# Moving the check of the weights from the vector engine to ScalarE, with new ordering offsets, in a fused attention and feed-forward kernel

## The chip, the core and the metric

The kernel runs on one core of a Trainium2 chip. The metric is the device time of one execution in microseconds (us), lower being better; the figure to compare is the median of repeated executions. The engines are named as in the profile: PE (TensorE, the matrix multiplies), PEld (its weight loads), DVE (the vector engine), ACT (ScalarE), POOL (GpSimd) and SP (SyncE, which here only issues transfers).

## The reference

There are two stages. The first is attention with four sink columns and a sliding window, for 4 batches, 8 heads, 768 positions and head size 64. The second is a feed-forward layer whose gate is a cosine, for 3072 tokens, width 512 and inner width 2048.

```python
scores = scale * q @ k.T
keep = (pos_k < n_sink) | ((rel >= 0) & (rel < window))      # n_sink 4, window 128
scores = where(keep, scores, -1e9)
a = exp(scores - max); a = a / (sum(a) + 1e-9)
x = (a @ v) with the heads of a token side by side           # 3072 x 512
h = x @ w_in                                                 # 512 x 2048
out = (h * cos(h)) @ w_out                                   # 2048 x 512
```

## The kernel before

**Tiles and stages.** The 3072 tokens are cut into 12 chunks of 256. A chunk has 8 heads of attention and then 8 slots of the feed-forward layer, each slot covering 256 of the 2048 inner columns. Precision beyond one pass of the multiplier is had by splitting numbers into a high and a low part: `h_mm` (L419) makes 24 multiplies for a slot and `out_mm` (L479) makes 12. Between them stands a chain that goes back and forth: `turns` on ACT (L428), `rest` on DVE (L434), `cosine` on ACT (L441, function Sin), `gate` on DVE (L446), `g_hi` on ACT (L458) and `g_lo` on DVE (L464). The heads have their own chain: `load_k` and `load_q` (L776, L763), `k_turn` on DVE (L879), the scores on PE (L906), `mask` on DVE (L919), `expo` on ACT (L928, function Exp with a summed output), `norm` (L951 on ACT, L953 on DVE or POOL), the transpose of the probabilities (L1021) and `values` on PE (L1101). Attention of later chunks is interleaved with the slots of earlier ones. The first three chunks have an opening in which weights are loaded and split and the first 24 heads use another form (L850, L1077), with filler multiplies (L1379) where PE has no other work.

**Order.** The order of all instructions on each engine is worked out while the program is built. Each step is entered in a `Plan` with the engines that can take it, an estimated duration, its dependencies and a due time; `order` then plays the engines forward and lets each take the ready step with the smallest due time. Due times are offsets held in the table `C`. For example, `DH` and `DM` place a slot's steps, `DQ`, `DS`, `DV` and `DX` the steps of a head, `SO` the splitting of `w_out`, `CK` the checks, and `PEN` is what a step is set back if it needs another ACT function table than the one loaded. Some steps may go to one of several engines (`norm`, some copies, the low parts). An engine then runs its instructions strictly in that order.

**The check.** The weights arrive as 64-bit floats and are turned to 32 bits by integer operations, which is right as long as no weight is very small. While the feed-forward layer runs, each of the 32 pieces of the weights (512 KB) is therefore read once more from memory into one of two `raw` buffers, and the upper words, read as 32-bit floats, are tested (`check_piece`, L595). One DVE instruction multiplies the 128 x 512 upper words with themselves and keeps the largest of the negated squares of each partition in a column of `tiny`. One check is entered for each slot after the first two chunks, due `CK` after it. In the end the columns are reduced (L1361) and compared with the limit `MIN_TOP * MIN_TOP`; where a weight is too small, a slow general path is run. It isn't run with these inputs. The two `raw` buffers also carry the output rows (`out_copy`, L407 and L409; `out_store`, L508), in an order fixed when the plan is made, and a load into one of them is issued by SP, which takes its transfers in order.

Of the kernel before, what the change touches and what calls it, by code (L numbers as in the profile page):

```python
# [9 lines left out]
F32 = mybir.dt.float32  # L10
F32R = mybir.dt.float32r
I32 = mybir.dt.int32
AF = mybir.ActivationFunctionType
ALU = mybir.AluOpType
PSUM = bass.MemoryType.PSUM

P = 128
# [8 lines left out]
MASKED = 8.0e9  # L26

C = {
# [3 lines left out]
    "NWF": 0.232, "PB": 5, "PEN": 27.684, "PL": 3, "POOLF": 4.428, "POOLPEN": -1.361, "QE": 5.937, "R": 2, "RAW": 2,  # L32
# [3 lines left out]
}  # L36
# [1 line left out]
MIN_TOP = 1.125 * 2.0**-15  # L38


def f32(ap):
    return ap.bitcast(F32)
# [7 lines left out]
class Plan:  # L50
# [8 lines left out]
    def buf(self, tag, n):  # L59
        row = self.bufs.setdefault(tag, [])  # L60
        row.append(Buf(row[len(row) - n] if len(row) >= n else None, len(row) % n))
        return row[-1]

    def add(self, engines, fn, deps, prio, lat=0.0, table=None, port=False):
        self.steps.append((engines, fn, deps, prio, lat, table))
        if port:
            self.port.add(len(self.steps) - 1)
        return len(self.steps) - 1
# [101 lines left out]
def attn_moe_kernel(ctx, tc, q, k, v, n_sink, window, w_in, w_out, out):  # L170
    nc = tc.nc
    B, H, S, D = q.shape
    w64 = w_in.dtype == mybir.dt.int64
    DM, DFF = w_in.shape
# [13 lines left out]
    NSLOT = NFT // FG  # L188
    WP = 2 * FG * P

    NEH = int(C["NEH"]) // 2 * 2
    NE = -(-NEH // H)
# [3 lines left out]
    cp = ctx.enter_context(tc.tile_pool(name="cp", bufs=1))  # L196
# [19 lines left out]
    rel, col = rc[:, 0], rc[:, 1]  # L216
    nw_i = cp.tile([P, 2, 2], I32, name="nw_i")
    nw4 = cp.tile([P, 2, 2], F32, name="nw4")
    neg3 = cp.tile([P, 3], F32, name="neg")
    neg, quarter = neg3[:, 0:2], neg3[:, 2:3]  # L220
    flag = cp.tile([1, 4], F32, name="flag")
    lims = cp.tile([1, 2, 2, 2], F32, name="lims")
    mine = cp.tile([GR, GQ], F32, name="mine")
    tiny = cp.tile([P, NC * NSLOT // 2 + NFT], F32, name="tiny")
    redo = cp.tile([1, 1], I32, name="redo")

    def setup():
        nc.vector.memset(quarter, HALF_PI_DOWN)
        nc.gpsimd.memset(ident, 0.0)
        nc.gpsimd.affine_select(  # L230
            out=ident, in_=ident, pattern=[[-1, P]], compare_op=ALU.not_equal, fill=1.0, base=0, channel_multiplier=1
        )
        nc.gpsimd.iota(rc_i[:, 0], pattern=[[-1, P]], base=0, channel_multiplier=1)
        nc.gpsimd.iota(rc_i[:, 1], pattern=[[1, P]], base=0, channel_multiplier=0)
        nc.gpsimd.memset(env.kz, 0.0)
        nc.gpsimd.memset(xb, 0.0)
        nc.gpsimd.memset(f32(env.vs), 0.0)

        for _ in range(C["WARM"]):
            nc.tensor.matmul(out=env.warm, lhsT=ident, rhs=ident, start=True, stop=True)  # L240
        nc.vector.memset(lims, 0.0)
        nc.vector.memset(lims[:, 0, 1, 0:1], 1.0)
        nc.vector.memset(lims[:, 1, 0, 0:1], float(NSINK))
        nc.vector.memset(lims[:, 1, 1, 0:1], float(P))
        nc.vector.tensor_single_scalar(out=minus, in_=ident, scalar=-1.0, op=ALU.mult)
        nc.vector.tensor_copy(out=rc, in_=rc_i)
        nc.vector.tensor_reduce(
            out=mine, in_=ident[:GR, :GR].rearrange("p (a h s) -> p h a s", a=2, h=GQ), axis=mybir.AxisListType.XY,
            op=ALU.max,
        )  # L250
# [261 lines left out]
    def dve(n, two=False, ptr=False):  # L512
        return ((n / 2 if two else n) + 62) / 960 + (0.06 if ptr else 0)

    def act(n, sbuf=True):
        return n / 1200 + (0.092 if sbuf else 0.051)
# [4 lines left out]
    def dma(n):  # L521
        return (("SP", 0.45 * n),)
# [50 lines left out]
    def split_piece(plan, prio, w, ready, before):  # L573


        add = plan.add

        def round_hi(e):
            nc.scalar.copy(out=w.high(), in_=w.w32)

        def rest_lo(e):
            e.tensor_tensor(out=w.low(), in0=w.w32, in1=f32(w.hi), op=ALU.subtract)  # L582

        s4 = add((("ACT", act(WP)),), round_hi, [ready], prio)
        return [s4, add(sub(WP), rest_lo, [s4, *before], prio, port=True)]

    def check_piece(plan, prio, k, w):

        add, buf = plan.add, plan.buf
        r = buf("raw", C["RAW"])  # L590
        raw = raws[r.nth]
        top = raw[:, :, 1].bitcast(F32)

        def least(e):
            nc.vector.tensor_tensor_reduce(  # L595
                out=top, in0=top, in1=top, op0=ALU.mult, op1=ALU.max, scale=-1.0, scalar=-3.0e38,
                accum_out=tiny[:, k : k + 1],
            )

        i = add(dma(1), lambda e: e.dma_start(out=raw.rearrange("p n w -> p (n w)"), in_=w.src), [r], prio - 6, lat=2.6)  # L600
        j = add((("DVE", dve(WP) + 0.02),), least, [i], prio, port=True)
        r.users += [i, j]
        return j

# [68 lines left out]
    def banded_path():  # L673
        plan = Plan()
        add, buf = plan.add, plan.buf
# [444 lines left out]
        i = add([("ACT", 1.9)], load_limits, [], -3000.0, lat=2.8)  # L1120
        i = add([("DVE", 0.6)], limits, [i], -3000.0, lat=0.1)
# [10 lines left out]
        def slot_time(a, s):  # L1132
            return C["S1"] + ((a - 1) * NSLOT + s) * T if a else C["S0"] + s * C["STEP"]

        slots = sorted((slot_time(a, s), a, s) for a in range(len(chunks)) for s in range(NSLOT))
# [222 lines left out]
        tmin = cp.tile([P, 2], F32, name="tmin")  # L1358
# [8 lines left out]
        def least_flag(e):  # L1367
            e.tensor_reduce(out=tmin[0:1, 1:2], in_=env.tm, axis=mybir.AxisListType.X, op=ALU.max)
            e.scalar_tensor_tensor(
                out=redo, in0=tmin[0:1, 1:2], scalar=-MIN_TOP * MIN_TOP, in1=flag[:, 0:1], op0=ALU.is_gt, op1=ALU.max  # L1370
            )

        idle = buf("b0", 1)
# [14 lines left out]
        for s in range(NSLOT):  # L1388
            t = slot_time(0, s)
# [5 lines left out]
        for m, (t, ss, w) in enumerate(sorted(pieces, key=lambda w: w[0])):  # L1395
            i = weight_piece(plan, t, w, guard=False, first=m < C["PL"])
# [16 lines left out]
        checks = [w for ws in w_ins for w in ws] if w64 else []  # L1413
        checks += w_outs if w64 else []
        checked = []
        nh = 0
        for t, a, s in slots:
            hs = ("b4", "b2") if a < NE - 1 else ("b4", "b2", "b3")
            hb = hs[nh % len(hs)]
            nh += 1  # L1420
            dense(plan, xs[a], a, s, t, T, w_in_ready, w_out_split if a else w_out_first, ACC, hb)
            for m in range(0 if a else FG):
                f = s * FG + m
                prio = slot_time(1, s) + C["SO"] + C["SO2"] * m
                pair = split_piece(plan, prio, w_outs[f], w_out_ready[s][f], before["out"])
                before["out"] = pair + xs[0].om[f]
                w_out_split.setdefault(s, []).append(pair[1])
            if a > 1 and len(checked) < len(checks):
                checked.append(check_piece(plan, t + C["CK"], len(checked), checks[len(checked)]))
        assert len(checked) == len(checks)  # L1430
        if w64:
            t = slots[8 + 2 * NSLOT + len(checks)][0]
            btp = buf("tp", 1)
            i = add([("DVE", 0.16)], least_all, checked, t)
            i = add([("PE", 0.13)], least_turn, [i, btp], t + 1.0)
            btp.users.append(add([("DVE", 0.4)], least_flag, [i], t + 2.0))

        emit(plan.order(BEGIN), setup)
        if not w64:
            nc.vector.tensor_copy(out=redo, in_=flag[:, 0:1])  # L1440
# [125 lines left out]
    with ExitStack() as ctx2:  # L1566
        x = banded_path()
# [37 lines left out]
```

## Time and profile before

| | us |
|---|---|
| median of three executions | 742.26 |
| lowest and highest of them | 742.24, 743.15 |
| the profiled execution's own time | 742.62 |
| its span, first to last instruction | 740.9 |
| PE busy in the span | 723.5 |
| DVE busy | 628.0 |
| ACT busy | 557.3 |
| POOL busy | 106.4 |

The span is shorter than the execution's own time by what lies ahead of the first and behind the last instruction. The granted TensorE clock is 0.999 of full speed over the span. Busy time of PE is a union of pipelined instructions whose ends are modelled, so that a short stall between two of them doesn't show in it.

### The profile page before, as it was taken

To read this page: it belongs to the slowest core of one execution; us is meant where nothing else is said; L and a number is where in the kernel's file an instruction comes from. 1 tells how busy PE (TensorE), PEld (TensorE's weight loads), DVE (VectorE), ACT (ScalarE), POOL (GpSimd) and SP (SyncE) were. 2 spreads that over 40 slices of the span, in tenths; PEclk is the share of its full clock that TensorE was granted. 3 is DMA by queue.
4 is the path that set the end of the run, shared out by engine and by line. 5 is a ranking of instruction groups with operands and counts; after the bars stand their busy time and mean duration, and the time that the engine had idled before them with its cause. 6 is when DMAs were issued, how large, how long until landed. Compare 5 with 4: busy or idle time off the path is not lost.

```text
span 740.9 us, 15107 instructions
## 1 busy us (share of the span) xinstructions
PE 723.5 (98%) x4827; PEld 644.0 (87%) x4827; DVE 628.0 (85%) x1778; ACT 557.3 (75%) x1387; POOL 106.4 (14%) x191
## 2 busy tenths in 40 slices
PE   8989999999999999999999999999999999999996
PEld 7777776799999998998998889999998999999995
DVE  6899999877899999999999999897988888965432
ACT  4889969556979778799797897887888697884422
POOL 1000000001121221212212122122001122212000
PEclk9999999999999999999999999999999999999999
DMA  5756565132355465465465442232242242110000
GB/s 151 199 170 187 160 183 167 55 49 41 97 141 132 98 148 138 96 170 121 113 157 158 93 107 53 56 67 43 51 89 48 41 85 49 34 41 7 31 1 32
DMA packets 215896, 71.48 MB, mean 96 GB/s; under 512 B 204288, under 2 KB 204800, under 8 KB 215808
## 3 DMA queue, kind: packets, MB, share of 16 engines
q1 hardware_dynamic: 215232, 70.17, 39.1%
q8 instruction: 40, 0.66, 0.4%
q14 instruction: 48, 0.39, 0.2%
q10 hardware_dynamic: 576, 0.26, 0.1%
HBM read 64.10 MB, written 6.29 MB: 95 GB/s over the span
## 4 chain that ended last, share of the span: by engine, by line
PE 77%; DVE 10%; ACT 8%; DMA 2%; issue 1%; SPq 0%; DVEq 0%; ACTq 0%
PE h L419 32%; PE acc L479 31%; PE av L1101 5%; PE s L906 4%; ACT p L928 2%; PE tp L1021 2%; ACT p L951 1%; DVE p L919 1%; DMA raw<-in_moe_w_in_dram 1%; DMA xq<-in_q_dram 1%; DVE w_out L546 1%; PE acc L474 1%; DVE w_out L552 1%; PE av L1077 1%; DVE lo_in L582 1%
## 5 line engine op out<-in xcount | busy, mean ns | idle before, releaser
L419 PE MATMUL h<-xhi,hi_in 128*128 128x256 f32 x768 | 226.0, 294 | 2.9 <-ACT firsts L407 1.5
L419 PE MATMUL h<-xlo,hi_in 128*128 128x256 f32 x768 | 217.0, 283 | 0.4 <-DVE xlo L365 0.4
L419 PE MATMUL h<-xhi,lo_in 128*128 128x256 f32 x768 | 216.8, 282 | 0.0
L419 PEld LDWEIGHTS h<-xhi,hi_in 128*128 128x128 f32 x768 | 146.0, 190 | 8.0 <-DVE glo L464 1.7
L419 PEld LDWEIGHTS h<-xhi,lo_in 128*128 128x128 f32 x768 | 146.3, 191 | 3.2 <-issue 1.1
L419 PEld LDWEIGHTS h<-xlo,hi_in 128*128 128x128 f32 x768 | 146.1, 190 | 0.6 <-DVE xlo L365 0.6
L479 PE MATMUL acc<-hi_out,ghi 128*128 128x512 f32 x350 | 142.3, 407 | 0.2 <-ACT raw L407 0.2
L479 PE MATMUL acc<-lo_out,ghi 128*128 128x512 f32 x350 | 137.4, 393 | 0.0
L479 PE MATMUL acc<-hi_out,glo 128*128 128x512 f32 x350 | 137.4, 393 | 0.0
L1060 POOL TENSOR_SCALAR_AFFINE_SELECT pz<-pz 128x512 fp32r<-128x512 f32 x128 | 83.4, 652 | 285.2 <-DVE pz L1047 212.4
L919 DVE CUSTOM_DVE_ANT_0 p<-s,mk 128x264 f32<-128x264 f32 (+1 forms) x192 | 75.5, 400 | 24.0 <-PE s L906 19.9
L428 ACT ACTIVATE yt<-h 128x512 int32<-128x512 f32 x96 | 57.2, 596 | 49.9 <-PE h L419 49.3
L928 ACT ACTIVATE p<-p,st 128x264 f32<-128x264 f32 (+1 forms) x192 | 93.6, 491 | 0.6
L434 DVE SCALAR_TENSOR_TENSOR r<-h,yt 128x512 f32<-128x512 f32 x96 | 65.4, 682 | 25.8 <-ACT yt L428 25.4
L441 ACT ACTIVATE r<-r,neg 128x512 f32<-128x512 f32 x96 | 69.3, 724 | 13.8 <-DVE r L434 13.0
L479 PEld LDWEIGHTS acc<-hi_out,glo 128*128 128x128 f32 x350 | 65.8, 188 | 14.9
L479 PEld LDWEIGHTS acc<-hi_out,ghi 128*128 128x128 f32 x350 | 65.9, 188 | 8.7 <-ACT raw L407 0.6
L479 PEld LDWEIGHTS acc<-lo_out,ghi 128*128 128x128 f32 x350 | 66.1, 189 | 7.6
L464 DVE TENSOR_TENSOR glo<-h,ghi 128x512 fp32r<-128x512 f32 x88 | 60.0, 682 | 11.5 <-ACT ghi L458 10.8
L446 DVE TENSOR_TENSOR h<-h,r 128x512 f32<-128x512 f32 x88 | 60.3, 686 | 8.2 <-ACT r L441 8.0
L458 ACT CAST ghi<-h 128x512 fp32r<-128x512 f32 x88 | 51.3, 583 | 16.1 <-PE acc L479 12.9
L906 PE MATMUL s<-r,l 128*128 128x264 f32 (+2 forms) x288 | 59.6, 288 | 0.8 <-DVE st L919 0.7
(140 smaller groups left out, 1285.0 us busy)
## 6 DMA issues: line engine op xcount, KB each, us to landing
raw<-in_moe_w_in_dram SPq DMA_DIRECT2D x32, 512.0 KB
raw<-in_moe_w_out_dram SPq DMA_DIRECT2D x32, 512.0 KB
xk<-in_k_dram SPq DMA_DIRECT2D x256, 48.0 KB
v<-in_v_dram SPq DMA_DIRECT2D x64, 96.0 KB
out_dram<-raw SPq DMA_DIRECT2D x22, 256.0 KB
xq<-in_q_dram SPq DMA_DIRECT2D x144, 32.0 KB
v<-in_v_dram SPq DMA_DIRECT2D x32, 64.0 KB
xq<-in_q_dram SPq DMA_DIRECT2D x24, 64.0 KB
```

The costliest lines, as they stand in the source:

```text
L419: nc.tensor.matmul(out=o.h[:, t, :], lhsT=w[:, fs], rhs=xx[:, c, :], start=(c == 0 and n == 0), stop=(c == NC - 1 and n == 2),)
L428: nc.scalar.activation(out=yt, in_=o.h, func=AF.Copy, scale=INV2PI, bias=0.25)
L434: nc.vector.scalar_tensor_tensor(out=o.r, in0=o.h, scalar=INV2PI, in1=yt, op0=ALU.mult, op1=ALU.subtract)
L441: nc.scalar.activation(out=o.r, in_=o.r, func=AF.Sin, scale=TWOPI_DOWN, bias=quarter)
L446: nc.vector.tensor_tensor(out=o.h, in0=o.h, in1=o.r, op=ALU.mult)
L458: nc.scalar.copy(out=o.ghi, in_=o.h)
L464: e.tensor_tensor(out=o.glo, in0=o.h, in1=f32(o.ghi), op=ALU.subtract)
L479: nc.tensor.matmul(out=x.acc[j], lhsT=gg[:, t, j * P : (j + 1) * P], rhs=w, start=(f == 0 and n == 0), stop=(f == NFT - 1 and n == 2), ski ...
L906: nc.tensor.matmul(out=o.s_ps[j][:, :w], lhsT=o.l[:, j * P : (j + 1) * P], rhs=r.rearrange("p n s -> p (n s)")[:, c0 : c0 + w], start=(n = ...
L919: nc.vector.tensor_tensor_reduce(out=o.p[:, j, :w], in0=o.s_ps[j][:, :w], in1=masks[min(o.i0 + j, 2)][:, :w], op0=ALU.add, op1=ALU.min, sc ...
L928: nc.scalar.activation(out=o.p[:, j, :w], in_=o.p[:, j, :w], func=AF.Exp, bias=o.lead.st[:, 0, o.nth, j : j + 1], scale=-1.0, accum_out=o. ...
L1060: nc.gpsimd.affine_select(out=env.pz4[:, :, :, n], in_=f32(env.pz4)[:, :, :, 0], pattern=[[0, 2], [0, CB], [sign, P]], compare_op=ALU.is_g ...
```

## The change

The check of a piece is now two ACT instructions in place of one DVE instruction. The first (`size`) squares the upper words in place. The second (`least`) computes the positive part of the limit minus the square and sums it over each partition into the column of `tiny`. The second is entered as depending on the first; both are entered for ACT alone. The limit lies in a new fourth column of the constant tile `neg`, set in `setup` by one more DVE memset. The final comparison is with 0 instead of the negated limit. The checks begin at the slot numbered `CN`, which is 16; in the order of due times this is the same slot as the first of the third chunk, at which they began before, and the final reduction is entered at the same slot. The check's own offset `CK` is unchanged. Seventeen other offsets have new values.

```diff
 C = {
-    "DH": -3.94, "DM": -1.983, "DQ": 6.389, "DS": -1.675, "DV": 3.174, "DX": 4.249, "E": [0.281, ...],
-    "LEAD": 0.258, "LP": -0.072, "NE": 0.037, "NW": 1.863, "NWF": 0.232, "PEN": 27.684,
-    "POOLF": 4.428, "POOLPEN": -1.361, "SAME": -0.554, "SO": 6.105,
+    "CN": 16, "DH": -4.269, "DM": -2.267, "DQ": 7.344, "DS": -1.79, "DV": 2.777, "DX": 3.832, "E": [0.22, ...],
+    "LEAD": 0.859, "LP": -0.247, "NE": 0.084, "NW": 1.512, "NWF": 0.237, "PEN": 9.884,
+    "POOLF": 4.199, "POOLPEN": -1.308, "SAME": -0.674, "SO": 10.829,
...
-    neg3 = cp.tile([P, 3], F32, name="neg")
+    neg3 = cp.tile([P, 4], F32, name="neg")
+    neg, quarter, floor = neg3[:, 0:2], neg3[:, 2:3], neg3[:, 3:4]
...
+        nc.vector.memset(floor, MIN_TOP * MIN_TOP)
...
+        def size(e):
+            nc.scalar.activation(out=top, in_=top, func=AF.Square)
         def least(e):
-            nc.vector.tensor_tensor_reduce(
-                out=top, in0=top, in1=top, op0=ALU.mult, op1=ALU.max, scale=-1.0, scalar=-3.0e38,
-                accum_out=tiny[:, k : k + 1],
+            nc.scalar.activation(
+                out=top, in_=top, func=AF.Relu, scale=-1.0, bias=floor, accum_out=tiny[:, k : k + 1]
             )
...
-        j = add((("DVE", dve(WP) + 0.02),), least, [i], prio, port=True)
+        j = add((("ACT", act(WP)),), size, [i], prio)
+        j = add((("ACT", act(WP) + 0.19),), least, [j], prio)
...
-                out=redo, in0=tmin[0:1, 1:2], scalar=-MIN_TOP * MIN_TOP, in1=flag[:, 0:1], op0=ALU.is_gt, op1=ALU.max
+                out=redo, in0=tmin[0:1, 1:2], scalar=0.0, in1=flag[:, 0:1], op0=ALU.is_gt, op1=ALU.max
...
-            if a > 1 and len(checked) < len(checks):
+            if n >= C["CN"] and len(checked) < len(checks):
```

## Rows read from the trace of the kernel before

**Rows 1.** First part of the page: busy us, share, instructions.

```profile
PE 723.5 (98%) x4827; PEld 644.0 (87%) x4827; DVE 628.0 (85%) x1778; ACT 557.3 (75%) x1387; POOL 106.4 (14%) x191
```

**Rows 2.** Stages: us, busy PE, PEld, DVE, ACT, POOL, clock, DMA share, GB/s.

```profile
0.00:60.00 60.00, 53.78 (x350) 45.99 (x351) 50.45 (x166) 42.66 (x125) 3.24 (x12) 1.00 0.61 175
...
200.00:440.00 240.00, 237.74 (x1662) 218.60 (x1661) 228.91 (x686) 199.21 (x505) 50.42 (x84) 1.00 0.54 130
440.00:650.00 210.00, 209.61 (x1463) 192.24 (x1462) 186.85 (x550) 171.98 (x431) 38.90 (x69) 1.00 0.30 58
```

**Rows 3.** Chain that ended last, pieces without gaps: start us, us, what.

```profile
276.96 0.60 PE av L1101 x7
...
278.33 0.24 PE s L906 x2
...
280.96 0.22 PE tp L1021 x2
...
686.48 7.19 PE h L419 x60
693.67 4.79 PE acc L479 x21
```

**Rows 4.** Groups of PE, 200 to 440 us: xcount, busy us, mean ns, idle.

```profile
L419 PE MATMUL h<-xhi,hi_in 128*128 128x256 f32 x272 | 79.6, 293 | 0.7 <-DVE glo L464 0.7
L479 PE MATMUL acc<-hi_out,glo 128*128 128x512 f32 x135 | 53.0, 393 | 0.0
L906 PE MATMUL s<-r,l 128*128 128x264 f32 x132 | 27.6, 291 | 0.7 <-DVE st L919 0.7
L1021 PE MATMUL tp<-ident,p 128*128 128x128 f32 x64 | 12.2, 272 | 0.0
L1101 PE MATMUL av<-gt,vs 128*128 128x256 f32 x33 | 9.3, 282 | 0.0
L1005 PE MATMUL gp<-ident,gc 128*64 128x128 f32 x16 | 3.0, 272 | 0.4 <-DVE gc L995 0.4
```

**Rows 5.** The same view of PE, 440 to 650 us.

```profile
L419 PE MATMUL h<-xhi,hi_in 128*128 128x256 f32 x236 | 68.8, 292 | 0.3 <-DVE glo L464 0.3
```

**Rows 6.** Groups of ACT: one of the whole span, then 200 to 440 us.

```profile
L579 ACT CAST hi_in<-w_in 128x512 fp32r<-128x512 f32 x16 | 9.8, 615 | 4.0 <-DVE w_in L552 3.9
...
L441 ACT ACTIVATE r<-r,neg 128x512 f32<-128x512 f32 x33 | 23.9, 724 | 4.0 <-DVE r L434 3.8
L951 ACT ACTIVATE p<-p,st 128x136 f32<-128x136 f32 x40 | 13.9, 400 | 1.0 <-DVE st L943 1.0
...
L441 ACT ACT_TABLE_LOAD x9 | 11.5, 1283 | 0.1
```

**Rows 7.** ACT in order of time: start us, us, instruction.

```profile
432.28 0.52 ACT L928 ACTIVATE p<-p,st 128x264 f32<-128x264 f32 x1
432.70 0.19 ACT L928 ACTIVATION_READ_ACCUMULATOR p<-p,st 128x1 f32 x1
432.79 0.51 ACT L928 ACTIVATE p<-p,st 128x264 f32<-128x264 f32 x1
```

**Rows 8.** Groups of DVE, 200 to 440 us.

```profile
L595 DVE CUSTOM_DVE_ANT_0 raw<-raw 128x512 f32<-128x512 f32 x32 | 21.7, 679 | 1.1 <-DMA raw<-in_moe_w_in_dram 1.0
L953 DVE TENSOR_SCALAR p<-p,st 128x136 f32<-128x136 f32 x11 | 2.8, 280 | 0.0
```

**Rows 9.** The chain again, where it leaves PE: start us, us, what.

```profile
287.47 3.18 DMA xk<-in_k_dram
...
422.62 1.64 DMA xk<-in_k_dram
```

**Rows 10.** SP's waits, 200 to 440 us: us in total, times, longest.

```profile
SPq L776 <- DVE tk L879: 29.9, 21, 5.9
SPq L600 <- DVE tiny L595: 5.2, 4, 3.3
```

**Rows 11.** Waits of the whole span.

```profile
DVE nw L258 <- DMA nw_i<-in_window_dram: 2.6, 1, 2.6
```

More of the change, by code (lines that the diff above doesn't have):

```diff
@@ L28 @@
 C = {
[3 rows of a table removed]
-    "NWF": 0.232, "PB": 5, "PEN": 27.684, "PL": 3, "POOLF": 4.428, "POOLPEN": -1.361, "QE": 5.937, "R": 2, "RAW": 2,
[1 row of a table removed]
[3 rows of a table added]
+    "NWF": 0.237, "PB": 5, "PEN": 9.884, "PL": 3, "POOLF": 4.199, "POOLPEN": -1.308, "QE": 5.937, "R": 2, "RAW": 2,
[1 row of a table added]
     "STEP": 7.406, "T": 7.838, "TE": [-0.711, 4.042, 6.076], "TQ": 4.813, "VE": 5.203, "WARM": 4, "WI": -8.99,
@@ L218, in attn_moe_kernel @@
     nw4 = cp.tile([P, 2, 2], F32, name="nw4")
-    neg3 = cp.tile([P, 3], F32, name="neg")
-    neg, quarter = neg3[:, 0:2], neg3[:, 2:3]
+    neg3 = cp.tile([P, 4], F32, name="neg")
+    neg, quarter, floor = neg3[:, 0:2], neg3[:, 2:3], neg3[:, 3:4]
     flag = cp.tile([1, 4], F32, name="flag")
@@ L1416, in banded_path @@
         nh = 0
-        for t, a, s in slots:
+        for n, (t, a, s) in enumerate(slots):
             hs = ("b4", "b2") if a < NE - 1 else ("b4", "b2", "b3")
@@ L1431, in banded_path @@
         if w64:
-            t = slots[8 + 2 * NSLOT + len(checks)][0]
+            t = slots[8 + int(C["CN"]) + len(checks)][0]
             btp = buf("tp", 1)
```

8 rows, old and new, of the table C are left out of this document.

## The prediction, made before the result was known

> **What bounds the kernel now.** I read the page's shares first: PE 98%, DVE 85%, ACT 75% [rows 1]. The check runs only from about 200 to 440 us, so the shares that count are those of that stage, which the table of stages gives: of 240 us DVE is busy for 228.9 (95%), ACT for 199.2 (83%), PE for 237.7 [rows 2]. DVE is nearly full there and ACT has 40.8 us left. After 440 us, without checks, DVE falls to 186.9 of 210 us (89%) and ACT stays at 82% [rows 2].
>
> A nearly full DVE costs time only if PE waits for it. PE's busy time can't say so, since the ends of its matmuls overlap. I therefore take the pitch of each kind of matmul from places where the chain runs on PE without a gap: 7.19/60 = 0.120 us for an h, 4.79/21 = 0.228 for an acc, 0.12 for an s, 0.60 for the seven of a head's av, 0.11 for a transpose [rows 3]. The check's stage holds 3 x 272 h, 3 x 135 acc (the other two kinds stand at 134 and 134), 132 s, 33 heads' av, 64 + 16 transposes [rows 4]: 97.8 + 92.4 + 15.8 + 19.8 + 8.8 = 234.6 us. So PE needs 234.6 of the 240 us, and all stalls together are about 5.4 us. A second view agrees that little is lost: 816 h in 240 us are 3.40 per us, and in the stage without checks 708 in 210 us are 3.37 [rows 4, 5]. Taking the check's work off DVE wholly could not bring more than those 5.4 us; PE bounds the stage otherwise.
>
> Where the stalls sit is told by the chain. Outside PE it passes through loads of k at 287 and 422 us, 3.18 and 1.64 us long [rows 9]. A load of k has to wait for the transpose on DVE that frees its buffer: SP stood 29.9 us in all for that in this stage [rows 10]. That is the place where a late DVE reaches PE: late transpose, late load, late scores.
>
> **The change part by part.**
>
> *Removed from DVE:* 32 instructions of 679 ns, 21.7 us [rows 8]. DVE goes from 228.9 to 207.2 us of 240, 86%, which is about its share after 440 us.
>
> *Added to ACT:* 32 squares and 32 summed positive parts. Neither stands in the trace. The nearest row for a square is a cast of 128 x 512 within SBUF, 615 ns; for the positive part, with its limit as a pointer operand, it is the Sin of 128 x 512, 724 ns [rows 6], and the reading of the sum, 0.19 us [rows 7]. Singly that is 615 + 724 + 190 = 1.53 us. But neighbours on ACT overlap: an Exp of 0.52 us and its reading of 0.19 take 0.51 us from one Exp to the next [rows 7], so about 0.1 us of each instruction lies under the next one. Three instructions with 0.1 us less each are 1.23 us. Bounds: 32 x 1.23 = 39 us if all overlap, 32 x 1.53 = 49 us if none does (the second ACT instruction needs the first one's output, so some won't). I take 40 us, as the plan can put another step between the two. ACT then goes from 199.2 to 239 of 240 us, 99.7%, if nothing else moves.
>
> *Moved in answer:* `norm` may run on DVE. 40 of them run on ACT in this stage, 13.9 us, at 400 ns each; DVE does one in 280 ns, 11.2 us for all 40 [rows 6, 8]. If all move, ACT is at 225 us (94%) and DVE at 218 (91%). I take about half. So the change roughly swaps the two engines' places: ACT gets the fullness that DVE had, and DVE some air.
>
> *The swap's worth.* What is queued behind a check on ACT is the Sin and the high parts of the slots, and the Exp of the heads. These chains have slack: in this stage PE's own gaps name DVE as the releaser in every PE row that has a gap [rows 4]. What is late on DVE, the transposes and masks, reaches PE over the k loads. With 21.7 us off DVE and up to 11 back, I give a bit more than half of the stage's 5.4 us back: -3.0 us, with bounds 0 (the pace is the same without checks) and -5.4.
>
> *The raw buffers.* A check holds its buffer until its last instruction. That is now two ACT instructions after the load, so 0.6 us longer at least. SP's load of a later piece waits for it, with k, q and v loads behind: so far 5.2 us of such waits in four places [rows 10]. I cost it at 0, because the checks are due 45 us after their slot and the loads ahead of that; the bound above is in the third rival.
>
> *The limit's memset, the final comparison.* One memset of one column more at the start. DVE waits 2.6 us there for the limits' transfer [rows 11], which covers it; without that cover it would be shorter than the 280 ns of the 136-column multiply [rows 8]. The final comparison has the same form. 0.
>
> *The offsets.* They reorder everything, the opening too, where PE is visibly idle for 6.2 of 60 us [rows 2]. No row says which way. Bounds: -6.2 if that idle time went, and as much the other way; value 0.
>
> **Sum.** 742.62 - 3.0 = 739.6 us by the profiled execution, which stands 0.36 us above the median; 739.3 as a median.
>
> **The rivals.** 0.2% is about what a measurement of this kernel can tell from no change; it is 1.5 us, so the borders are 740.8 and 743.7.
>
> *Nothing happens to the end (same).* PE needs its 234.6 us anyway, and the stage's remaining stalls come from order, not from load. For it: the equal pace with and without checks [rows 4, 5]. Against it: the chain leaves PE for transfers that wait on DVE [rows 9, 10]. About 742.
>
> *ACT becomes the bound (slower).* One mechanism: ACT in the check's stage. From 199.2 us it takes 40.8 more before it is full. At 1.23 us a check it just fits; at 1.53 us it needs 248 us, 8 over, and every microsecond over is one of PE's. It decides from 1.28 us a check on (40.8/32), unless `norm` moves. Its signs would be late buffers: loads held at SP behind an unfinished check, late output copies, late Sins. With half of the `norm`s moved the worst is 248 - 7 = 241, but table loads of 1.28 us [rows 6] and batches of Exp come in lumps, and ACT, unlike DVE, has these. I price it at 3 to 8 us above the profiled run: 745 to 750. The Trainium skill speaks for this rival: "ScalarE: Activation LUTs", section "Rules for kernel authors", sends relu and multiplication to the vector engine, not to ScalarE. The trace agrees in sum, in so far as 40 us of ACT by neighbouring rows stand against 21.7 us of DVE; by that rule the kernel ends slower.
>
> *The new functions need a table load.* An Exp or a Sin after the other costs 1.28 us [rows 6]. If Square had to be loaded each time, it would be 32 x 1.28 = 41 us on a full ACT, about 780 us. Against it: casts and copies run between Sins with no load of their own. The same page, section "Table sets: the hidden batching unit", says that cheap functions, relu among them, stand in every set; it doesn't list Square there, and no run shows it yet.
>
> *The offsets shorten the opening.* Up to the 6.2 us of idle time: 733 to 736. No row speaks for it.
>
> **How the numbers follow.** Forecast (736 to 740.8) 0.46; nothing happens 0.24; ACT the bound 0.23; table loads 0.02; a shorter opening 0.05. Faster is 0.46 + 0.05 = 0.51, same 0.24, slower 0.25. The range goes from 735.5, the stage's full 5.4 us with a little of the opening, to 746.5, which takes in a good half of the slower case; outside lie the shorter opening (0.05), the slower case's far end (0.10) and the table loads (0.02), 0.17 in all. The forecast's own range is 736 to 740.8.
>
> **What would show it.** In the profile of the changed kernel: no DVE instruction of the check; DVE near 90% and ACT at 94 to 99% from 200 to 440 us; a Square near 0.62 us, a positive part near 0.72 with 0.19 behind it; about as many table loads as before; fewer `norm`s on ACT; shorter waits of SP for the k transpose, and no chain through k loads. It would be wrong if PE waited for Sin, Exp or high parts in that stage, if the waits of SP for the check grew beyond 5 us, if check pieces slipped far past 440 us with the output copies behind them, or if the time moved before 200 us, where no check runs.

## The result, and the profile after

The changed kernel takes 749.5 us in the median, 742.3 before: a ratio of 1.0094, 95% interval 1.0080 to 1.0109. It is slower by about 7 us; 739.3 was predicted, with a range to 746.5 and a chance of 0.25 for slower.

The first part of the page of the changed kernel [rows 1]:

```profile
PE 727.8 (97%) x4827; PEld 643.6 (86%) x4827; DVE 617.1 (82%) x1735; ACT 595.8 (80%) x1465; POOL 105.5 (14%) x191
```

Its stages, with the columns of [rows 2]:

```profile
0.00:60.00 60.00, 54.33 (x350) 46.64 (x351) 50.47 (x167) 42.68 (x125) 3.25 (x12) 1.00 0.62 175
...
200.00:440.00 240.00, 234.60 (x1614) 211.06 (x1613) 212.71 (x627) 229.42 (x566) 49.29 (x83) 1.00 0.53 130
440.00:650.00 210.00, 209.60 (x1464) 192.43 (x1464) 187.01 (x549) 173.90 (x437) 36.93 (x70) 1.00 0.30 57
```

The opening and the stage from 440 us are as before. The stage of the check has changed: DVE from 228.9 to 212.7 us, ACT from 199.2 to 229.4 (96%), and PE got through 1614 matmuls in it in place of 1662. The loss lies there.

The chain of work that ended last says by what. Its shares of the span by engine, before and then after, and two of its pieces after (start us, us, what):

```profile
PE 77%; DVE 10%; ACT 8%; DMA 2%; issue 1%; SPq 0%; DVEq 0%; ACTq 0%
```

```profile
PE 66%; ACT 16%; DVE 12%; issue 3%; DMA 2%; SPq 1%; POOL 0%; DVEq 0%; ACTq 0%; POOLq 0%
```

```profile
236.14 0.57 ACT raw L596
236.74 0.86 ACT raw L599 x2
```

ACT's share has doubled, and the check itself now stands in the chain: from 200 to 440 us L599 has 4.8% of it and L596 4.2%, together some 22 us. The loads of k have 2.6%.

Groups of ACT in that stage [rows 6]; L596 is the square, L599 the positive part with its summed output:

```profile
L599 ACT ACTIVATE raw<-raw,neg 128x512 f32<-128x512 f32 x31 | 24.0, 774 | 0.7
...
L596 ACT ACTIVATE raw<-raw 128x512 f32<-128x512 f32 x31 | 21.0, 677 | 4.0 <-DMA raw<-in_moe_w_in_dram 2.9 <-DMA raw<-in_moe_w_out_dram 1.0
...
L442 ACT ACT_TABLE_LOAD x8 | 10.3, 1283 | 0.1
...
L955 ACT ACTIVATE p<-p,st 128x136 f32<-128x136 f32 x27 | 9.1, 396 | 0.0
L599 ACT ACTIVATION_READ_ACCUMULATOR raw<-raw,neg 128x1 f32 x31 | 5.9, 190 | 0.0
```

Neither new function brought a table load (8 loads under Sin where there were 9), and 13 of the 40 `norm`s left ACT. What the reader is to see is the gap column of the square: ACT stood 2.9 us at the head of its queue for one transfer of the check.

SP's waits in the stage [rows 10] have turned round:

```profile
SPq L603 <- ACT raw L599: 16.2, 9, 2.9
SPq L780 <- DVE tk L883: 12.9, 10, 2.7
```

The wait for DVE's transpose of k fell from 29.9 to 12.9 us, as forecast (whether by DVE's relief, e6 below tells). The wait of the check's loads for the check rose from 5.2 us in four places to 16.2 in nine, and PE came out behind. Its groups there [rows 4] have larger gaps, with other tiles of the same chains as releasers:

```profile
L420 PE MATMUL h<-xhi,hi_in 128*128 128x256 f32 x264 | 77.2, 292 | 1.3 <-DVE glo L465 1.2
...
L910 PE MATMUL s<-r,l 128*128 128x264 f32 x130 | 28.4, 296 | 2.1 <-DVE l L877 1.0 <-DVE st L923 0.8 <-DVE r L901 0.2
```

### The profile page after: what moved, and what is told of

Read it like the earlier page. It is cut to its first block, busy times and chain, and to the rows that moved or that the text cites. A ratio compares the mean times of both kernels' runs of the same rounds, so it can differ in the third digit from the quotient of the medians.

```text
span 748.0 us, 15119 instructions
## 1 busy us (share of the span) xinstructions
PE 727.8 (97%) x4827; PEld 643.6 (86%) x4827; DVE 617.1 (82%) x1735; ACT 595.8 (80%) x1465; POOL 105.5 (14%) x191
## 4 chain that ended last, share of the span: by engine, by line
PE 66%; ACT 16%; DVE 12%; issue 3%; DMA 2%; SPq 1%; POOL 0%; DVEq 0%; ACTq 0%; POOLq 0%
PE h L420 27%; PE acc L480 25%; PE av L1105 4%; PE s L910 4%; ACT r L442 2%; ACT p L932 2%; ACT p L955 2%; ACT raw L599 2%; PE idle L1383 1%; PE tp L1025 1%; ACT raw L596 1%; DVE p L923 1%; ACT yt L429 1%; ACT L442 1%; ACT r L895 1%
## 5 line engine op out<-in xcount | busy, mean ns | idle before, releaser
L447 DVE TENSOR_TENSOR h<-h,r 128x512 f32<-128x512 f32 x88 | 60.8, 690 | 10.4 <-ACT r L442 10.2
```

The source lines that it names most:

```text
L447: nc.vector.tensor_tensor(out=o.h, in0=o.h, in1=o.r, op=ALU.mult)
```

## The experiments

Three theories were to be told apart: ScalarE's load costs the time; the check's transfers and the waits for them do; the order that the offsets give does. Each run was timed against the kernel before; the ratio is the figure to compare between runs.

| run | median us | ratio to before, 95% interval |
|---|---|---|
| the changed kernel | 749.5 | 1.0094 (1.0080 to 1.0109) |
| e1 check on ScalarE, old offsets | 755.6 | 1.0180 (1.0159 to 1.0201) |
| e2 check on the vector engine, new offsets | 753.3 | 1.0146 (1.0129 to 1.0163) |
| e3 no arithmetic of the check, old offsets | 755.3 | 1.0191 (1.0169 to 1.0213) |
| e4 no arithmetic of the check, new offsets | 760.1 | 1.0248 (1.0224 to 1.0271) |
| e5 order of the changed kernel, short check | 743.9 | 1.0027 (1.0016 to 1.0037) |
| e6 order of before, short check | 742.3 | 1.0001 (0.9987 to 1.0016) |
| e7 as e5, small loads too | 740.6 | 0.9977 (0.9966 to 0.9988) |
| e8 before, checks due 1 us later | 745.9 | 1.0045 (1.0029 to 1.0062) |
| e9 as e5, only the second instruction short | 745.6 | 1.0053 (1.0039 to 1.0068) |
| e10 as e6, small loads too | 742.2 | 1.0001 (0.9989 to 1.0013) |
| e11 changed kernel, checks 24 slots later | 751.8 | 1.0133 (1.0110 to 1.0156) |
| e12 before, checks 24 slots later | 751.0 | 1.0110 (1.0084 to 1.0136) |
| e13 order of e1, short check | 750.7 | 1.0113 (1.0077 to 1.0150) |
| e14 order of e2, short check | 751.7 | 1.0128 (1.0099 to 1.0158) |
| e15 before, preparation of heads due 0.1 us later | 747.6 | 1.0072 (1.0047 to 1.0097) |
| e16 changed kernel, Exp due 0.1 us later | 753.7 | 1.0158 (1.0123 to 1.0193) |

### Each engine with each set of offsets

```diff
 e1: the changed kernel, with
-    "DH": -4.269, "DM": -2.267, ... "PEN": 9.884, ... "SO": 10.829
+    "DH": -3.94, "DM": -1.983, ... "PEN": 27.684, ... "SO": 6.105
 e2: the kernel before, with the same lines the other way round
 e3, e4: the kernel before, and the changed one, each with
-        j = add(..., least, [i], prio, ...)
+        # no step: the load alone uses the buffer; tiny is set once in setup
```

> The check on ScalarE as in the change, with all offsets as before the change. If the load on ScalarE costs the time: 747 to 752 us, ScalarE at 94 to 98% from 200 to 440 us. If the new offsets cost it: 740 to 744 us.

> The check on the vector engine as before, with the seventeen new offsets. If the load on ScalarE costs the time: 740 to 744 us, like the kernel before. If the new offsets cost it: 747 to 752 us.

> The kernel before with the check's arithmetic left out; its 32 loads remain and the column tile is set once. It gives what 21.7 us off the vector engine are worth by themselves. If the prediction's gain was sized right: 738 to 740 us. If PE's own need bounds that stage: 741 to 743 us.

> The changed kernel with the check's arithmetic left out on ScalarE; its 32 loads remain. If the load on ScalarE costs the time: 738 to 743 us, the whole loss of 7 us comes back. If the offsets or the loads' waits cost it: 746 to 750 us.

Measured: 755.6, 753.3, 755.3 and 760.1 us. No theory held. The old offsets with the new check are slow, the new offsets with the old check are slow as well, and without any arithmetic of the check the kernel is as slow with the old set (755.3) and slower still with the new one (760.1). So a time can't be read off an engine's load here: leaving a step out also changes the order of everything after it.

What such an order does is seen best where work was left out. In e4 nothing holds a `raw` buffer but its transfer, so the plan let the check's loads follow one another. SP's instructions in order of time (start us, us):

```profile
326.52 5.77 SPq L604 DMA_DIRECT2D raw<-in_moe_w_out_dram  x4
332.38 1.92 SPq L779 DMA_DIRECT2D xk<-in_k_dram  x4
```

And a piece of its chain, and its stages with the columns of [rows 2]:

```profile
333.83 4.30 DMA xk<-in_k_dram
```

```profile
335.00:340.00 5.00, 0.88 (x3) 0.50 (x2) 1.84 (x5) 0.31 (x2) 0.00 (x0) 0.84 0.77 146
340.00:345.00 5.00, 4.67 (x22) 4.62 (x23) 4.54 (x14) 2.08 (x5) 1.48 (x3) 0.50 0.72 220
345.00:350.00 5.00, 5.00 (x44) 5.00 (x44) 2.69 (x10) 2.04 (x6) 1.27 (x2) 0.97 0.35 64
```

Four loads of 512 KB keep SP for 5.8 us, with a stand of 3.2 us between the second issue and the third; the load of k is issued behind them and its last piece lands 4.3 us after its issue; PE is busy for 0.9 of the 5 us from 335. This one place costs over 4 us, with an emptier DVE, and more by the clock (last section).

### The order held fixed, the load taken away

An instruction's width in the program need not be the duration that the plan counts with. Cutting the check to 8 of 512 columns leaves the order of every engine the same, instruction for instruction (the traces of e5, e6, e7, e9 and e10 show it), and takes only the load away.

```diff
 e5 (changed kernel), e6 (before):
-        top = raw[:, :, 1].bitcast(F32)
+        top = raw[:, :8, 1].bitcast(F32)
 e7 (e5) and e10 (e6) also:
-        e.dma_start(out=raw..., in_=w.src)
+        e.dma_start(out=raw...[:, :16], in_=w.src[:, :16])
 e9 (changed kernel), the second instruction alone:
-        nc.scalar.activation(out=top, in_=top, func=AF.Relu, ...)
+        nc.scalar.activation(out=top[:, :8], in_=top[:, :8], func=AF.Relu, ...)
```

> The changed kernel in its own order, instruction for instruction; only the two check instructions work on 8 columns of each piece in place of 512, so that most of the check is left out and about 1 us of each of the 32 pieces leaves ScalarE. If ScalarE's load makes the changed kernel slow: 740 to 744 us. If its order or the loads in it do: 747 to 750 us.

> The kernel before in its own order; the vector engine's check works on 8 columns of each piece, which leaves most of the check out and takes about 0.5 us of each of the 32 pieces from the vector engine. If relief of the vector engine is worth what the prediction took: 739 to 740 us. If it is worth nothing without a new order: 741 to 743 us.

> As the run with the changed kernel's order and the short check, and the loads of the check also cut to 16 words of each row (8 KB in place of 512 KB), so that the check is left out but for 8 columns. If the check's transfers hold up the loads of k behind them: 2 us or more below the run with the short check alone. If not: the same as that.

> The changed kernel in its own order, with the square whole and only the positive part cut to 8 columns (which leaves most of the comparison out). Half of the load that the short check took off ScalarE is back. If the cost follows the load evenly: 746 to 747.5 us, between 743.9 and 749.5. If it begins only when ScalarE is nearly full: 743.5 to 745 us.

> The kernel before in its own order, with the check on 8 columns and its loads cut to 8 KB, so that nearly all of the check is left out, arithmetic and transfer. If the check's transfers cost time in that order as they did in the changed one: 738 to 740 us. If PE bounds that order anyway: 741 to 743 us.

Measured: e5 743.9, e6 742.3, e7 740.6, e9 745.6, e10 742.2 us. The stage from 200 to 440 us of e5, and then of e9, e7 and e6, columns as in [rows 2]:

```profile
200.00:440.00 240.00, 236.88 (x1655) 216.64 (x1654) 216.04 (x645) 209.55 (x585) 49.64 (x84) 1.00 0.55 132
```

```profile
200.00:440.00 240.00, 235.10 (x1631) 213.60 (x1631) 213.61 (x636) 219.41 (x576) 49.85 (x84) 1.00 0.55 130
```

```profile
200.00:440.00 240.00, 238.65 (x1670) 219.27 (x1669) 218.94 (x660) 212.46 (x591) 49.46 (x86) 1.00 0.34 63
```

```profile
200.00:440.00 240.00, 237.72 (x1663) 218.84 (x1662) 215.77 (x688) 199.02 (x505) 49.39 (x85) 1.00 0.55 130
```

*ScalarE's load* is worth 5.6 us in the changed kernel's order (749.5 to 743.9; by the ratios 0.67%, 5.0 us): ACT at 209.6, 219.4 and 229.4 us gives 743.9, 745.6 and 749.5. e9 falls between the two cases of its expectation: whether the cost rises evenly can't be said, as the middle of the two outer ratios, 1.0061, lies in e9's interval. It costs before ACT is full, since e9, with ACT at 91% of the stage, is already clear of e5 with 87%. PE's instructions have the same order in these traces, so their starts can be compared one by one: the changed kernel is level with e5 to within 0.5 us up to 230 us, then falls behind in many steps of 0.6 us at most, and stands 5.3 us behind from 440 us on. A shorter check also gives its buffer back earlier: SP's wait for it is 16.2 us in the changed kernel, 10.6 in e9 and 7.0 in e5. How much of the 5.6 us reaches PE over ACT's queue and how much over SP these runs don't part.

*The check's transfers* cost another 3.2 us in that order (743.9 to 740.6), taken off with the check already short; with the whole check they were not taken off alone. In the two traces 2.9 us of the difference arise after 200 us, and 2.5 of these at one place, from 300 to 309 us. The chain of the changed kernel shows that place. Its pieces on ACT and DVE between two stretches of PE:

```profile
303.18 0.76 PE acc L480 x3
...
303.96 0.39 ACT l L870
304.35 0.43 ACT r L895
304.78 0.49 ACT yt L429
...
305.29 1.28 ACT L442
...
306.59 0.72 ACT r L442
...
308.25 0.73 ACT r L442
308.98 0.48 ACT ghi L459
...
309.49 0.70 DVE glo L465
...
310.23 0.98 PE h L420 x6
```

All this stood behind the square of a check that waited for its load. ACT in order of time, with the idle time before the instruction and its releaser in brackets:

```profile
303.40 0.66 ACT L596 ACTIVATE raw<-raw 128x512 f32<-128x512 f32 x1 [2.93 <-DMA raw<-in_moe_w_in_dram]
```

With the check short the same chain begins with that load (e5):

```profile
297.58 4.27 DMA raw<-in_moe_w_in_dram
```

With small loads (e7) the chain runs on PE alone from 298 to 312 us.

*The vector engine's relief* is worth nothing: e6 is at 742.3 us with 13.1 us less on DVE in the stage, e10 at 742.2 with the transfers gone as well. The stalls are the same ones: from 200 us on the starts of PE's instructions in the two traces stay within 0.2 us of each other. PE's waits from 285 to 445 us in the kernel before, and then in e6 (us in total, times, longest):

```profile
PE h L419 <- DVE glo L464: 1.0, 2, 0.7
PE s L906 <- DVE st L919: 0.7, 2, 0.5
PE h L419 <- DVE xlo L365: 0.4, 1, 0.4
PE gp L1005 <- DVE gc L995: 0.4, 1, 0.4
```

```profile
PE h L419 <- DVE glo L464: 1.0, 2, 0.7
PE s L906 <- DVE st L919: 0.7, 2, 0.5
PE gp L1005 <- DVE gc L995: 0.4, 1, 0.4
PE h L419 <- DVE xlo L365: 0.4, 1, 0.4
```

SP's wait for the transposes of k, 29.9 us before [rows 10], is as long in e6, so DVE's check was not what made it long:

```profile
SPq L776 <- DVE tk L879: 29.6, 20, 5.7
```

The load of k that stood in the chain at 287 us [rows 9] has left it in e6; the chain goes over ACT in its place and comes to the same end. The load itself came no earlier: it is issued at 287.34 us in e6 and at 287.47 before, and all of e6 runs 0.13 us ahead there. Before, and then e6:

```profile
290.68 0.42 DVE x L1115
...
292.64 0.73 ACT r L441
...
297.11 0.38 PE gp L1005 x2
```

```profile
291.22 0.92 ACT L441
...
292.51 0.73 ACT r L441
...
296.98 0.38 PE gp L1005 x2
```

Before, the chain goes from the load to L1115, which adds `av` and `xb` and doesn't read k. In e6 that instruction starts at 290.47 us, and the Sin behind it on ACT is only 0.13 us earlier, like all the rest.

### How much an order is worth

```diff
 e8 (before):            -"CK": 45.316  +"CK": 46.316
 e15 (before):           -"DQ": 6.389   +"DQ": 6.489
 e16 (changed kernel):   -"DX": 3.832   +"DX": 3.932
 e11 (changed kernel):   -"CN": 16      +"CN": 40
 e12 (before):           -if a > 1 and len(checked) < len(checks):
                         +if n >= 40 and len(checked) < len(checks):   # and the final step 24 slots later
 e13 (e1), e14 (e2):     the short check of e5, in the order of e1 and of e2
```

> The kernel before, check on the vector engine, with one offset moved: the checks are due 46.316 us after their slot in place of 45.316. The work and the transfers are the same; the order of all engines comes out anew. If the time follows engine load: 741 to 744 us. If it follows how well the offsets fit this one order: 746 to 756 us.

> The kernel before with the loads and preparation of the heads due 0.1 us later (DQ 6.489 in place of 6.389); the work is the same and the order comes out anew. If a new order with unfitted offsets costs time whatever its cause: 745 us or more. If small changes of the order don't matter: 741 to 743 us.

> The changed kernel with the Exp steps due 0.1 us later (DX 3.932 in place of 3.832); the work is the same and the order comes out anew. If the new offsets are fitted to the changed kernel's order: 751 us or more. If its order is no better than its neighbours: 747 to 751 us.

> The changed kernel with the checks beginning at slot 40 in place of 16, so that they run from about 390 to 640 us, where the other transfers leave more room and ScalarE was 82% busy. The order comes out anew. If ScalarE's load is what costs, it costs the same there: 746 to 756 us. If the place of the transfers matters more: 740 to 745 us.

> The kernel before with the vector engine's checks beginning at slot 40 in place of 16 and its offsets as they are. The order comes out anew. If the vector engine's fullness or the transfers in the stage from 200 to 440 us cost time: 738 to 741 us. If a new order with unfitted offsets costs more than that: 744 to 752 us.

> The order of the run with the check on ScalarE and the old offsets (755.6 us), instruction for instruction; only the check works on 8 columns, so most of it is left out. If ScalarE's load makes that order slow as it does the changed one: 748 us or less, at least 6 us back. If that order is bad by itself: 752 to 756 us.

> The order of the run with the check on the vector engine and the new offsets (753.3 us); only the check works on 8 columns, so most of it is left out. If the vector engine's fullness makes that order slow: 748 us or less. If that order is bad by itself: 751 to 754 us.

Measured: e8 745.9, e15 747.6, e16 753.7, e11 751.8, e12 751.0, e13 750.7, e14 751.7 us. An offset moved by 0.1 us, with the work unchanged, costs 5 us on the kernel before and 4 us on the changed one. All three neighbours tried are slower, two of the kernel before and one of the changed one, so both sets of offsets look fitted, each to its own kernel; e8 fell just short of the range for that. Moving the checks to a stage with more room (e11, e12) gave nothing, but those are new orders too and don't tell what a fitted one would give. e13 splits the 13.6 us of e1 and lies between the two cases of its expectation: 4.9 us go with ScalarE's load, a second time about 5; 8.1 us stay with the order. Its interval is 2.7 us wide to either side. In e14 only 1.6 of e2's 11 us go with the vector engine's load, and the intervals overlap.

## Why the prediction was wrong, point by point

*PE bounds the stage; the gain is at most 5.4 us.* Borne out as far as tested. With the check nearly gone, arithmetic and transfer, the two orders take 742.2 (e10) and 740.6 us (e7).

*DVE falls by the check, ACT takes 40 us, some `norm`s move.* Right in the profile: DVE at 212.7, ACT at 229.4 us, inside the 225 to 239. Singly the instructions are longer than taken, 677 and 774 ns for 615 and 724; but the 31 checks of the stage fill only 40.3 us in which ACT does nothing else, 1.30 us each for the 1.25 taken. The Trainium skill, "ScalarE: Activation LUTs", section "What ACT_TABLE_LOAD costs", puts a pointer operand at about 93 ns. Here the instruction that has one takes 97 ns more than the one without; it also sums its output, so the 97 ns are not the operand's for certain.

*The swap's worth, -3.0 us.* This step failed first. It took the two loads of k in the chain, and SP's waits for the transpose, as signs that a late DVE holds PE up. In the changed kernel those waits were more than halved, and the time rose; its chain still passes through loads of k (4.52 us at 226.52). In e6 DVE had its relief in an unchanged order, and SP's waits and every stall of PE stayed. The load of k at 287 us was no cause: the instruction that the chain hung on it doesn't read k, and with it 0.2 us earlier the next releaser was as late as before, ACT's Sin and `norm`s, which stand in a fixed order. The term measures 0 (ratio 1.0001, 0.9987 to 1.0016; -3.0 us would be 0.9960) in the order of before. What relief is worth in an order fitted to it was not measured.

*"These chains have slack", ACT at 94 to 99% without a cost.* The second step that failed. It read slack on ACT from rows of PE that name DVE as the releaser. But the `glo` named there is the last step of a chain that comes from ACT, as its own row from 200 to 440 us of the kernel before says:

```profile
L464 DVE TENSOR_TENSOR glo<-h,ghi 128x512 fp32r<-128x512 f32 x33 | 22.5, 680 | 1.4 <-ACT ghi L458 1.2
```

The rival had it: ACT the bound, 745 to 750 us, at a chance of 0.23, with 749.5 measured. The rule that it named from "ScalarE: Activation LUTs" of the Trainium skill, "Rules for kernel authors", agrees with the outcome. Its mechanism was half right: the point of decision, 1.28 us a check, was just passed with 1.30, but `norm`s moved, ACT ended at 96%, not over, and the load cost 5 us all the same. It asked for a full ACT; e9 shows a cost at 91%.

*The raw buffers at 0.* Wrong by 3.2 us in this order: a check's load that lands late stops ACT (2.9 us at 303 us), and what stands behind it waits. A late check holds SP too, but of those 16.2 us 9.2 go with the arithmetic (e5) and count in its term. The bound that this step refers to stands in the second rival, not the third.

*The offsets at 0, bounded by the opening's 6.2 us of idle time.* Wrong place and wrong size. The opening didn't move (PE busy 54.3 of 60 us, 53.8 before). Offsets act where PE is full, by the order in which ACT, DVE and SP take their steps, and are worth some 10 us there (e2: 11 us).

*The sum as it turned out:* 740.6 (the changed kernel's order, check short, loads small) + 3.2 (the loads) + 5.6 (ScalarE's load) = 749.4 us, for 749.5 measured. For the kernel before: 742.2 + 0 + 0. The terms are steps from run to run, so the sum closes by construction. The new offsets gave an order that would be 1.6 us better if the check cost nothing; the loss is the check's price on ScalarE in it, arithmetic and transfers. By the measured ratios the terms' uncertainty is about 1 us each.

*Open:* what the best order for the check on ScalarE would take. Fitting was not tried; seventeen offsets moved at once here. Why e1 and e2 are as slow as they are was followed only to the split in e13 and e14 and to the clock (last section). No version that does the whole check and beats the kernel before was found, and e10 says that in its order none of the check's cost is left to gain.

## What to carry to other kernels

Before an engine's relief is priced, take its work away with the order held fixed (cut the width, keep the plan's numbers): here 13 us less on a 95% full engine bought nothing. In a kernel with an order worked out from fitted offsets, a change is compared with its own fitted order only; the unfitted orders here cost 3 to 18 us of 742, where the change cost 7. Work that waits for a transfer stops all that stands behind it in its engine's queue: here the check with its loads cost nothing measurable on DVE, 95% busy, and 8.8 us on ACT, 96% busy, each in its own order.

## What the runs showed of the hardware that had not been expected

In e4 TensorE stood for over 4 us from 335 us (busy 0.88 of 5 us). The granted clock was 0.84 over those 5 us, 0.50 over the next 5, in which TensorE worked again, and 0.97 over the 5 after them: that stall was paid for again at the lower of the two levels, 1.2 in place of 2.4 GHz. The stage rows of that run above show it. e4 has two more such places, at 287 and 400 us, and 13.6 us at 0.50 in all between 200 and 440 us; e1 has 6.8 us, e3 10.2 and e13 6.8. At half the clock at most half of such a time is lost, so by estimate up to 6.8 us of e4's 18, and up to 3.4 of the 8.1 us that e13 leaves to the order, are clock. In the profiled executions of the kernel before, the changed kernel, e5 to e10, e15 and e16 the clock stayed at 1.00 through the stage, so it explains none of their differences there.
